# The first groups of a dense layer in wavefront order instead of three passes, with weight conversion paced to use (mLSTM cell and shrink layer, one core)

## The chip, the cores and the metric

The kernel runs on one core of a Trainium2 chip. A core has a matrix engine (TensorE, PE in the profile, with its weight loads as PEld), VectorE (DVE), ScalarE (ACT), GpSimd (POOL) and SyncE (SP), which here only issues transfers. Each engine works through its own list of instructions in order and waits on semaphores for the others. The metric is the device time of one execution in microseconds (us).

## The reference

An mLSTM cell runs over 4 batches, 8 heads, 768 steps and head size 40; its output, 3072 tokens of 320 features, goes through a dense layer with 2048 hidden features and the activation `h - tanh(h)`.

```python
for t in range(S):
    m_new = np.maximum(f_gate[:, :, t] + m, i_gate[:, :, t])
    f_stab = np.exp(f_gate[:, :, t] + m - m_new)
    i_stab = np.exp(i_gate[:, :, t] - m_new)
    C = f_stab * C + i_stab * einsum('bhd,bhe->bhde', v_t, k_t)
    n = f_stab * n + i_stab * k_t
    y[:, :, t] = sigmoid(o_gate_t) * (C @ q_t) / max(|n . q_t|, 1)
x = y.transpose(0, 2, 1, 3).reshape(B * S, H * D)   # 3072 x 320
h = x @ w_in                                        # 320 x 2048, float64 in memory
out = (h - tanh(h)) @ w_out                         # 2048 x 320, float64 in memory
```

All arithmetic on the chip is float32. The two weight matrices lie in memory as float64 bits and are turned into float32 on the chip.

## The kernel before

**Units.** The recurrence is done in chunks of 128 steps. A unit is one chunk of one batch, all heads: 24 units, numbered so that the four batches of a chunk follow each other. `cell_slot(s, o, x)` (line 435) makes a list of small steps for three units at once: unit `s` is fetched ahead, its decay matrix `E` is made by a scan on DVE (`decay`, line 341), and its scores are multiplied on PE into `ps` and from there by DVE into `E` (`score`, line 375); unit `o` gets its output `ph` from the state and from `E` (`inter`, `intra`), a state update `pc` (`update`, line 410) with DVE, and its output gate on DVE (`gate`, line 398); unit `x` is transposed on PE into `px` and copied by ACT into `xT` (`turn`, line 425). `prepare` (line 353) runs before an output: GpSimd scales `v` into `vs` and `q` into `qg`. `ph`, `pc` and `px` share one pool of two PSUM buffers (`ps_b`). The list `slots` (line 539) says which units a slot takes: normally `s`, `s-2` and `s-3`. There are 27 slots; a full one has all three units.

**Dense items.** Two units make a group of 256 tokens (12 groups); 256 hidden features make a weight pair (8 pairs). An item is one group with one pair: 96 items. `up(g, p)` (line 471) does six products into `ph_up` and the activation (two ACT and two DVE instructions into `gt`). `down(g, p, first, last)` (line 494) multiplies `gt` with `w_out` into the two accumulators `po`; it is issued `LAG` = 2 items after its `up`. `first` and `last` bound the run of pairs that one accumulation covers. At a run's end `evict` takes `po` out: ACT copies a group's first run into `part`, DVE adds later runs to `part`, and the last one goes to `ob` and to memory. Each of the two `po` has one buffer, so the next run's first product into it waits for that.

**Conversion.** `weights` (line 260) turns one float64 block into float32 in five pieces: a fetch by SP into the staging tile `w64` (six buffers); a mask and a shift on DVE (lines 282, 285); three ACT conversions (283, 286, 287); an add and a multiply on GpSimd (288, 289); and the sign on DVE (293). A pair has five blocks (three of `w_in`, two of `w_out`), 40 in all. `convert` (line 300) puts them into steps: step n fetches block n, does the middle of block n-2 and the sign of block n-4.

**Order.** PE's order is the order in which the program writes its products (`T.keep`). `merge` (line 523) interleaves two lists of steps in proportion to the costs that stand beside them. On the other engines the compiler orders the instructions by the program's order and its own estimate of when each is ready, so that a ready conversion can be put ahead of its place. The list before is in three passes over the first six groups: pairs 0 and 1 for groups 0 to 5, then pairs 2 to 4, then pairs 5 to 7; groups 6 to 11 then run all eight pairs each.

```python
PASSES = ((0, 1), (2, 4), (5, NP - 1))
```

Four slots and the conversion of pairs 0 and 1 (14 steps) come ahead of the first item. Slots 4 to 16 lie in items 0 to 11, together with the conversion of pairs 2 to 4; that of pairs 5 to 7 is laid over items 12 to 28; slots 17 to 26 lie in items 33 to 83.

Of the kernel before, what the change touches and what calls it, by code (L numbers as in the profile page):

```python
# [33 lines left out]
I64 = mybir.dt.int64  # L37
# [23 lines left out]
def kernel(  # L61
# [16 lines left out]
    class T:  # L78

        last = None  # L80
# [16 lines left out]
    B, NT, D, H, _ = qT.shape  # L97
# [4 lines left out]
    KC = [(c, min(128, DM - c)) for c in range(0, DM, 128)]  # L102
    NK = len(KC)
    NU = B * NT
    GT = 2
    TG = GT * L
    NG = NU // GT
    NP = NFF // 2
    HH = H // 2
    LAG = 2  # L110
    FIRST = 6
    NX = FIRST + 1
    PASSES = ((0, 1), (2, 4), (5, NP - 1))

    const = ctx.enter_context(tc.tile_pool(name="const", bufs=1))
    load = ctx.enter_context(tc.tile_pool(name="load", bufs=2))
# [2 lines left out]
    conv = ctx.enter_context(tc.tile_pool(name="conv", bufs=2))  # L119
# [85 lines left out]
    for w in (after, ones):  # L205
        p = ps_b.tile([w.shape[1], NT, BH], FP, name="psum_lf", tag="b")
# [12 lines left out]
    xr, n, f = (mlp.tile([L, 2, NR], FP, name=name, tag=tag) for name, tag in (("xr", "z"), ("n", "z"), ("f", "q")))  # L219
# [40 lines left out]
    def weights(dst, src):  # L260

        p, n = dst.shape
        w = {}

        def fetch():
            if src.dtype == FP:
                nc.sync.dma_start(out=dst, in_=src)
                return
            w["st"] = conv.tile([128, n], I64, name="w64", tag="w64", bufs=6)[0:p]
            nc.sync.dma_start(out=w["st"], in_=src)  # L270

        def magnitude():
            if src.dtype == FP:
                return
            hi = w["hi"] = w["st"].bitcast(I32).rearrange("p (n two) -> p n two", two=2)[:, :, 1]
            lo = w["st"].bitcast(U32).rearrange("p (n two) -> p n two", two=2)[:, :, 0]
            e = conv.tile([128, n], I32, name="w_e", tag="w_e")[0:p]
            m = conv.tile([128, n], I32, name="w_m", tag="w_m")[0:p]
            r = w["r"] = conv.tile([128, n], I32, name="w_r", tag="w_r", bufs=4)[0:p]
            mf, rf = m.bitcast(FP), r.bitcast(FP)  # L280

            V.tensor_single_scalar(e, hi, 0x7FF00000, op=OP.bitwise_and)  # L282
            A.activation(out=e, in_=e, func=AF.Relu, scale=8.0, bias=rebias[0:p])  # L283

            V.tensor_single_scalar(m, hi, 12, op=OP.logical_shift_left)  # L285
            A.activation(out=mf, in_=m.bitcast(U32), func=AF.Copy, scale=2.0 ** -32, bias=1.0)  # L286
            A.activation(out=rf, in_=lo, func=AF.Copy, scale=2.0 ** -52)
            G.tensor_tensor(out=rf, in0=rf, in1=mf, op=OP.add)  # L288
            G.tensor_tensor(out=rf, in0=rf, in1=e.bitcast(FP), op=OP.mult)  # L289

        def sign():
            if src.dtype != FP:
                V.scalar_tensor_tensor(out=dst.bitcast(I32), in0=w["hi"], scalar=-(1 << 31), in1=w["r"],  # L293
                                       op0=OP.bitwise_and, op1=OP.bitwise_or)

        return fetch, magnitude, sign

    WB = 2 * 128

    def convert(pairs):  # L300

        blocks = []
        for p in pairs:
            cols = slice(p * WB, (p + 1) * WB)
            for c, (r0, rows) in enumerate(KC):
                blocks.append(weights(w_in[0:rows, c, cols], moe_w_in[r0:r0 + rows, cols]))
            for f in (2 * p, 2 * p + 1):
                blocks.append(weights(w_out[:, f, :], moe_w_out[f * 128:(f + 1) * 128, :]))
        steps = []
        for x in range(len(blocks) + 4):  # L310
            def step(x=x):
                for late, part in enumerate((0, None, 1, None, 2)):
                    if part is not None and 0 <= x - late < len(blocks):
                        blocks[x - late][part]()
            steps.append((1.0, step))
        return steps


    xT = [const.tile([128, NK, TG], FP, name=f"xT{i}") for i in range(NX)]
    part = [const.tile([L, DM], FP, name=f"part{i}") for i in range(FIRST * GT)]  # L320

# [103 lines left out]
    def turn(n, j):  # L425
# [4 lines left out]
        if j == NK - 1:  # L430
            g, tt = divmod(n, GT)
            A.copy(out=xT[g % NX][:, :, tt * L:(tt + 1) * L], in_=t["px"])  # L432
            un.pop(n)

    def cell_slot(s, o, x):


        steps = []

        def begin():  # L440
            if o is not None:
                prepare(o)
            if s is not None and s - 1 in un:
                prepare(s - 1)
            if s is not None:
                if s + 1 < NU:
                    fetch(s + 1)
                decay(s)

        steps.append((0.0, begin))  # L450
        for d in range(HH):
            for i in range(2):
                if s is not None:
                    steps.append((0.22, lambda h=2 * d + i: score(s, h)))
                if o is not None and i == 0:
                    steps.append((0.22 if o >= B else 0.0, lambda d=d: inter(o, d)))
            if o is not None:
                steps += [(0.22, lambda h=h: intra(o, h)) for h in (2 * d, 2 * d + 1)]
                if d in (1, 2) and o + B < NU:
                    steps += [(0.18, lambda j=j: update(o, j)) for j in (2 * d - 2, 2 * d - 1)]  # L460
        if o is not None:
            steps.append((0.0, lambda: gate(o)))
        if x is not None:
            steps += [(0.11, lambda j=j: turn(x, j)) for j in range(NK)]
        return steps
# [57 lines left out]
    def merge(a, b):  # L523

        total = [sum(cost for cost, _ in x) or 1.0 for x in (a, b)]
        done, at = [0.0, 0.0], [0, 0]
        while at[0] < len(a) or at[1] < len(b):
            i = int(done[1] / total[1] < done[0] / total[0])
            if at[i] == len((a, b)[i]):
                i = 1 - i  # L530
            cost, step = (a, b)[i][at[i]]
            done[i] += cost
            at[i] += 1
            step()
# [1 line left out]

    slots = [(0, None, None), (1, 0, None), (2, 1, 0), (3, None, 1)]
    AHEAD = len(slots)  # L540
    slots += [tuple(n if lo <= n < NU else None for n, lo in ((s, 0), (s - 2, 2), (s - 3, 2)))
              for s in range(AHEAD, NU + 3)]
    NS = len(slots)

    def slots_for(g):

        return AHEAD if g == 0 else GT * g + 5

    items = []
    starts = {}  # L550
    for first, last in PASSES:
        for g in range(FIRST):
            starts[g, first] = len(items)
            items += [(g, p, first, last) for p in range(first, last + 1)]
    for g in range(FIRST, NG):
        starts[g, 0] = len(items)
        items += [(g, p, 0, NP - 1) for p in range(NP)]


    work = [[] for _ in range(len(items) + LAG)]  # L560

    def spread_over(steps, x0, x1):

        for i, step in enumerate(steps):
            work[int(x0 + i * (x1 - x0) / len(steps))].append(step)

    def pairs_of(i):
        return range(PASSES[i][0], PASSES[i][1] + 1)

    for g in range(FIRST):  # L570
        x0, now, then = starts[g, 0], slots_for(g), slots_for(g + 1)
        for i in range(now, then):
            n = len(pairs_of(0))
            spread_over(cell_slot(*slots[i]), x0 + (i - now) * n / (then - now), x0 + (i + 1 - now) * n / (then - now))
    for i in range(1, len(PASSES)):
        spread_over(convert(pairs_of(i)), starts[0, PASSES[i - 1][0]], starts[0, PASSES[i][0]] - 1)
    late = range(slots_for(FIRST), NS)
    x0, x1 = starts[1, PASSES[-1][0]], starts[NG - 1, 0] - HH
    for i, n in enumerate(late):
        spread_over(cell_slot(*slots[n]), x0 + (x1 - x0) * i / len(late), x0 + (x1 - x0) * (i + 1) / len(late))  # L580

    blocks = convert(pairs_of(0))
    spread(ld[0].setdefault("E", att.tile([L, H, L], FP, name="E", tag="E", bufs=4)), f_rows, 0, slice(0, H))
    for i in range(AHEAD):
        merge(cell_slot(*slots[i]), blocks[i * len(blocks) // AHEAD:(i + 1) * len(blocks) // AHEAD])
    for x in range(len(items) + LAG):
        dense = up(*items[x][:2]) if x < len(items) else []
        if x >= LAG:
            dense = dense + down(*items[x - LAG])
        merge(dense, work[x])  # L590


    most = att.tile([128, 1], FP, name="most", tag="most")
# [6 lines left out]
    lead, root, _, rest = POLY  # L600
# [17 lines left out]
    with tc.If(nc.values_load(again, min_val=0, max_val=128,  # L618
                              skip_runtime_bounds_check_because="it counts partitions") > 0):
        T.last = None  # L620
        for g in range(NG):
# [16 lines left out]
            x = xT[g % NX]  # L638
# [59 lines left out]
```

## Time and profile before

| what | us |
|---|---|
| median of 4 runs (lowest, highest) | 681.49 (679.31, 682.75) |
| the profiled execution, its time | 678.71 |
| the profiled execution, its span | 677.0 |
| PE busy, share of the span | 607.3, 90% |
| DVE busy, share | 365.4, 54% |
| ACT busy | 220.2 |
| POOL busy | 152.0 |
| first product of item 0, of item 12, of item 33, of item 84 | 59.93, 209.12, 323.35, 608.90 |

The profile is of one execution. Its span runs from the first to the last instruction; the execution's own time is 1.7 us longer. Matrix products are pipelined, so a busy PE is not one at its peak. The row of slices cuts the span in 40 parts of 16.9 us; a digit is the busy share in tenths, and PEclk is the clock that TensorE was granted, in tenths of full speed. In a line of a group of instructions, the numbers after the first bar are the busy time in us and the mean duration of one in ns, those after the second the time its engine stood idle right before these instructions and what ended most of it. In a line of the timeline, the first number is the start in us, the second how long the merged instructions last, and the bracket an idle time before them and its releaser.

### The profile page before, as it was taken

To read this page: it belongs to the slowest core of one execution; us is meant where nothing else is said; L and a number is where in the kernel's file an instruction comes from. 1 tells how busy PE (TensorE), PEld (TensorE's weight loads), DVE (VectorE), ACT (ScalarE), POOL (GpSimd) and SP (SyncE) were. 2 spreads that over 40 slices of the span, in tenths; PEclk is the share of its full clock that TensorE was granted. 3 is DMA by queue.
4 is the path that set the end of the run, shared out by engine and by line. 5 is a ranking of instruction groups with operands and counts; after the bars stand their busy time and mean duration, and the time that the engine had idled before them with its cause. 6 is when DMAs were issued, how large, how long until landed. Compare 5 with 4: busy or idle time off the path is not lost.

```text
span 677.0 us, 8514 instructions
## 1 busy us (share of the span) xinstructions
PE 607.3 (90%) x3100; PEld 504.3 (74%) x3100; DVE 365.4 (54%) x609; ACT 220.2 (33%) x511; POOL 152.0 (22%) x171
## 2 busy tenths in 40 slices
PE   1296889889899849999999999999999999999996
PEld 1295868778788637878888888888888888878784
DVE  8787888886887983333353635344333332332321
ACT  2333153243324743232232323222232322242331
POOL 7654355346354770000010101101010000000000
PEclk9757889899999979999999999999999999999999
DMA  5555765555344520000030402112000000000000
GB/s 156 174 159 178 214 187 148 160 153 157 119 134 140 167 86 1 0 1 0 20 99 29 133 13 93 56 36 79 1 11 19 1 1 19 1 21 0 20 0 25
DMA packets 46210, 50.97 MB, mean 75 GB/s; under 512 B 3984, under 2 KB 38416, under 8 KB 46160
## 3 DMA queue, kind: packets, MB, share of 16 engines
q1 hardware_dynamic: 42288, 46.22, 22.8%
q10 hardware_dynamic: 3872, 4.13, 1.8%
q8 instruction: 26, 0.43, 0.2%
q14 instruction: 24, 0.20, 0.1%
HBM read 46.20 MB, written 4.13 MB: 74 GB/s over the span
## 4 chain that ended last, share of the span: by engine, by line
PE 68%; DVE 15%; POOL 9%; issue 3%; ACT 3%; ACTq 0%; POOLq 0%; DVEq 0%
PE ph_up L91 32%; PE po L91 27%; DVE E L350 4%; PE ph L91 4%; PE ps L91 3%; POOL w_r L289 3%; POOL w_r L288 3%; DVE w_in L293 2%; DVE E L381 2%; DVE w_e L282 1%; ACT w_e L283 1%; DVE gt L489 1%; DVE w_out L293 1%; PE pc L91 1%; DVE w_m L285 1%
## 5 line engine op out<-in xcount | busy, mean ns | idle before, releaser
L91 PE MATMUL ph_up<-xT,w_in 128*128 128x256 f32 x1152 | 301.8, 388 | 5.5 <-ACT xT L432 3.7
L91 PE MATMUL po<-w_out,gt 128*128 128x320 f32 x768 | 246.8, 446 | 10.2 <-DVE part L508 8.5
L91 PEld LDWEIGHTS ph_up<-xT,w_in 128*128 128x128 f32 x1152 | 206.1, 192 | 38.9 <-ACT xT L432 5.4
L91 PEld LDWEIGHTS po<-w_out,gt 128*128 128x128 f32 x768 | 138.4, 194 | 48.1 <-DVE part L508 9.8
L489 DVE SCALAR_TENSOR_TENSOR gt<-ph_up,z 128x512 f32<-128x512 f32 x96 | 66.0, 688 | 198.2 <-ACT z L487 198.1
L487 ACT ACTIVATE z<-ph_up 128x512 f32<-128x512 f32 x96 | 57.2, 596 | 317.9 <-PE ph_up L91 316.1
L91 PE MATMUL ps<-q,kz 128*128 128x128 f32 x384 | 80.5, 309 | 11.1 <-DVE E L381 10.8
L91 PEld LDWEIGHTS ps<-q,kz 128*128 128x128 f32 x384 | 69.8, 215 | 18.9 <-DVE E L381 11.1
L490 DVE SCALAR_TENSOR_TENSOR gt<-q,gt 128x512 f32<-128x512 f32 x96 | 68.2, 710 | 9.0 <-ACT q L488 1.7
L91 PEld LDWEIGHTS ph<-vs,E 128*128 128x128 f32 x384 | 66.6, 205 | 7.5
L488 ACT ACTIVATE q<-z,tiny 128x512 f32<-128x512 f32 x96 | 69.2, 721 | 2.7
L350 DVE TENSOR_TENSOR_SCAN E<-E,diag 128x1024 f32<-128x1024 f32 x24 | 59.5, 2484 | 3.2 <-DMA E<-f_rows 3.2
L91 PE MATMUL ph<-vs,E 128*128 128x41 f32 x384 | 59.8, 261 | 0.0
L366 POOL TENSOR_TENSOR qg<-qg,q 80x512 f32<-80x512 f32 x20 | 26.2, 1311 | 138.3 <-DMA qg<-g_rows 138.3
L370 POOL TENSOR_TENSOR state<-state,eT 80x328 f32<-80x328 f32 x16 | 13.6, 849 | 158.1 <-PE ph L91 98.7
L381 DVE TENSOR_TENSOR E<-ps,E 128x512 f32<-128x512 f32 x48 | 32.8, 684 | 20.8 <-PE ps L91 19.3
L288 POOL TENSOR_TENSOR w_r<-w_r,w_m 128x256 f32<-128x256 f32 (+2 forms) x40 | 33.5, 837 | 41.3 <-ACT w_m L286 34.5
L289 POOL TENSOR_TENSOR w_r<-w_r,w_e 128x256 f32<-128x256 f32 (+2 forms) x40 | 36.3, 907 | 2.4
L91 PEld LDWEIGHTS ph<-state,qg 128*128 128x128 f32 x160 | 28.9, 194 | 5.8 <-POOL state L370 0.6
L293 DVE SCALAR_TENSOR_TENSOR w_in<-w,w_r 128x256 int32<-128x256 int32 (+1 forms) x24 | 25.8, 1074 | 13.5 <-POOL w_r L289 13.5
L95 PE MATMUL px<-ident,ys 128*128 128x128 f32 x72 | 16.1, 290 | 18.2 <-DVE state L421 14.2
L363 POOL TENSOR_TENSOR vs<-v,ei 128x640 f32<-128x640 f32 (+1 forms) x24 | 28.5, 1188 | 1.1 <-ACT z L487 0.5
(89 smaller groups left out, 356.4 us busy)
## 6 DMA issues: line engine op xcount, KB each, us to landing
E<-f_rows SPq DMA_DIRECT2D x24, 512.0 KB
w<-in_moe_w_out SPq DMA_DIRECT2D x16, 320.0 KB
w<-in_moe_w_in SPq DMA_DIRECT2D x16, 256.0 KB
kz<-in_kT SPq DMA_DIRECT2D x48, 80.0 KB
q<-in_qT SPq DMA_DIRECT2D x48, 80.0 KB
v<-in_v SPq DMA_DIRECT2D x24, 160.0 KB
k<-in_k SPq DMA_DIRECT2D x24, 160.0 KB
o<-in_o_gate SPq DMA_DIRECT2D x24, 160.0 KB
```

What stands on the lines that cost most here:

```text
L91: return cls.keep(nc.tensor.matmul(*args, **kwargs))
L288: G.tensor_tensor(out=rf, in0=rf, in1=mf, op=OP.add)
L289: G.tensor_tensor(out=rf, in0=rf, in1=e.bitcast(FP), op=OP.mult)
L293: V.scalar_tensor_tensor(out=dst.bitcast(I32), in0=w["hi"], scalar=-(1 << 31), in1=w["r"], op0=OP.bitwise_and, op1=OP.bitwise_or)
L350: V.tensor_tensor_scan(out=row, data0=row, data1=diag.rearrange("p h t -> p (h t)"), initial=0.0, op0=OP.mult, op1=OP.add)
L363: G.tensor_tensor(out=t["vs"][:, both, :, 0:D], in0=t["v"].unsqueeze(1).to_broadcast(shape), in1=scale.unsqueeze(3).to_broadcast(shape), o ...
L366: G.tensor_tensor(out=t["qg"][0:TOP], in0=t["qg"][0:TOP], in1=t["q2"][0:TOP], op=OP.mult)
L381: V.tensor_tensor(out=P, in0=t["ps"], in1=P, op=OP.mult)
L487: A.activation(out=z, in_=ph, func=AF.Square, accum_out=sums[:, g * NP + p:g * NP + p + 1])
L488: A.activation(out=q, in_=z, func=AF.Square, bias=tiny)
L489: V.scalar_tensor_tensor(out=gt, in0=ph, scalar=TINY_POLY[0], in1=z, op0=OP.mult, op1=OP.mult)
L490: V.scalar_tensor_tensor(out=gt, in0=q, scalar=TINY_POLY[2], in1=gt, op0=OP.add, op1=OP.mult)
```

## The change

The first four groups take the place of the first six. The list of items is written out as stages; each is a list of runs (group, first pair, last pair) and the number of cell slots laid over them. A new pair is used for all groups that are there, and a new group runs over all pairs that are there: item 0 is group 0 with pair 0, then group 0 with pair 1, group 1 with pairs 0 and 1, pair 2 for groups 0 and 1, and so on up to item 31. Groups 0 to 3 have 7, 6, 4 and 3 runs; before, six groups had three each. Groups 4 to 11 run all eight pairs each, as groups 6 to 11 did.

The slots are filled differently at the start: unit 2's output moves from slot 4 into slot 3, ahead of item 0, unit 3's into slot 4, and slot 5 has none. Slots 4 to 13 lie in the stages, 14 to 26 evenly over items 32 to 83, four items each. The conversion is one chain of 44 steps over all pairs. Nine steps, up to the end of pair 0, come ahead of item 0; five for each further pair are spread between the due times of the pair before and its own. Worked out, pair 1 is converted over item 0, pair 2 over items 1 and 2, pair 3 over 3 to 5.5, pair 4 over 5.5 to 11.5, pair 5 to 18, pair 6 to 20.5 and pair 7 to 27.5. Within an item, steps of cell and conversion are sorted by their place. The staging tile has eight buffers for six, there are six `xT` tiles for seven, and eight `part` tiles for twelve.

```diff
-    FIRST = 6
-    NX = FIRST + 1
-    PASSES = ((0, 1), (2, 4), (5, NP - 1))
+    STAGES = (
+        ([(0, 0, 0)], 2),
+        ([(0, 1, 1), (1, 0, 1)], 0),
+        ([(0, 2, 2), (1, 2, 2)], 1),
+        ([(0, 3, 3), (1, 3, 3)], 2),
+        ([(2, 0, 3)], 0),
+        ([(0, 4, 4), (1, 4, 4), (2, 4, 4)], 2),
+        ([(3, 0, 4)], 0),
+        ([(0, 5, 6), (1, 5, 6), (2, 5, 6), (3, 5, 6)], 2),
+        ([(0, 7, 7), (1, 7, 7), (2, 7, 7), (3, 7, 7)], 1),
+    )
+    FIRST = 4
+    NX = FIRST + 2
...
-            w["st"] = conv.tile([128, n], I64, name="w64", tag="w64", bufs=6)[0:p]
+            w["st"] = conv.tile([128, n], I64, name="w64", tag="w64", bufs=8)[0:p]
...
-    slots = [(0, None, None), (1, 0, None), (2, 1, 0), (3, None, 1)]
-    AHEAD = len(slots)
-    slots += [tuple(n if lo <= n < NU else None for n, lo in ((s, 0), (s - 2, 2), (s - 3, 2)))
-              for s in range(AHEAD, NU + 3)]
+    slots = [(0, None, None), (1, 0, None), (2, 1, 0), (3, 2, 1), (4, 3, 2), (5, None, 3), (6, 4, None)]
+    AHEAD = 4
+    slots += [tuple(n if n < NU else None for n in (s, s - 2, s - 3)) for s in range(len(slots), NU + 3)]
...
-    for first, last in PASSES:
-        for g in range(FIRST):
-            starts[g, first] = len(items)
+    for runs, _ in STAGES:
+        for g, first, last in runs:
             items += [(g, p, first, last) for p in range(first, last + 1)]
+    START = len(items)
...
+    x, done = 0, AHEAD
+    for runs, n in STAGES:
+        x1 = x + sum(last - first + 1 for _, first, last in runs)
+        for i in range(n):
+            spread_over(cell_slot(*slots[done]), x + i * (x1 - x) / n, x + (i + 1) * (x1 - x) / n)
+            done += 1
+        x = x1
+    x1 = (NG - 1 - FIRST) * NP - HH
+    for i in range(done, NS):
+        spread_over(cell_slot(*slots[i]), START + x1 * (i - done) / (NS - done), START + x1 * (i + 1 - done) / (NS - done))
...
+    steps = convert()
+    ready = [len(KC) * p + 2 * p + len(KC) + 2 + 4 for p in range(NP)]
+    due = [0.0, 1.0] + [min(i for i, item in enumerate(items) if item[1] == p) - 0.5 for p in range(2, NP)]
+    for p in range(NP - 2, 0, -1):
+        due[p] = max(min(due[p], due[p + 1] - 2.5), 1.0)
+    for p in range(1, NP):
+        spread_over(steps[ready[p - 1]:ready[p]], due[p - 1], due[p])
+
+    first = steps[:ready[0]]
...
-        merge(dense, work[x])
+        merge(dense, [(cost, step) for _, cost, step in sorted(work[x], key=lambda w: w[0])])
```

More of the change, by code (lines that the diff above doesn't have):

```diff
@@ L298, with convert @@
     WB = 2 * 128
-    def convert(pairs):
+    def convert():
         blocks = []
-        for p in pairs:
+        for p in range(NP):
             cols = slice(p * WB, (p + 1) * WB)
@@ L534, in merge @@
             step()
-    slots = [(0, None, None), (1, 0, None), (2, 1, 0), (3, None, 1)]
-    AHEAD = len(slots)
-    slots += [tuple(n if lo <= n < NU else None for n, lo in ((s, 0), (s - 2, 2), (s - 3, 2)))
-              for s in range(AHEAD, NU + 3)]
+    slots = [(0, None, None), (1, 0, None), (2, 1, 0), (3, 2, 1), (4, 3, 2), (5, None, 3), (6, 4, None)]
+    AHEAD = 4
+    slots += [tuple(n if n < NU else None for n in (s, s - 2, s - 3)) for s in range(len(slots), NU + 3)]
     NS = len(slots)
-    def slots_for(g):
-        return AHEAD if g == 0 else GT * g + 5
     items = []
-    starts = {}
-    for first, last in PASSES:
-        for g in range(FIRST):
-            starts[g, first] = len(items)
+    for runs, _ in STAGES:
+        for g, first, last in runs:
             items += [(g, p, first, last) for p in range(first, last + 1)]
+    START = len(items)
     for g in range(FIRST, NG):
-        starts[g, 0] = len(items)
         items += [(g, p, 0, NP - 1) for p in range(NP)]
@@ L562, in spread_over @@
     def spread_over(steps, x0, x1):
[L564 to L582, printed above, removed]
+        for i, (cost, step) in enumerate(steps):
+            at = x0 + i * (x1 - x0) / len(steps)
+            work[int(at)].append((at, cost, step))
+    x, done = 0, AHEAD
[16 more added lines that the diff above has]
+    first = steps[:ready[0]]
     spread(ld[0].setdefault("E", att.tile([L, H, L], FP, name="E", tag="E", bufs=4)), f_rows, 0, slice(0, H))
     for i in range(AHEAD):
-        merge(cell_slot(*slots[i]), blocks[i * len(blocks) // AHEAD:(i + 1) * len(blocks) // AHEAD])
+        merge(cell_slot(*slots[i]), first[i * len(first) // AHEAD:(i + 1) * len(first) // AHEAD])
     for x in range(len(items) + LAG):
```

## The prediction

> **What bounds the kernel now.** I read the page's shares and its row of 40 slices first, then the busy times by stretch, then the groups of instructions by shape, last the timeline of PE. The shares alone mislead: PE is busy 90% of the span, VectorE (DVE) 54%.
>
> ```profile
> PE 607.3 (90%) x3100; PEld 504.3 (74%) x3100; DVE 365.4 (54%) x609; ACT 220.2 (33%) x511; POOL 152.0 (22%) x171
> ...
> PE   1296889889899849999999999999999999999996
> ...
> DVE  8787888886887983333353635344333332332321
> ...
> PEclk9757889899999979999999999999999999999999
> ```
>
> The rows show two regimes: up to about slice 15 (250 us) DVE is at eight to nine tenths and PE has holes; from there PE is full and DVE has a third. So I cut the span where items of the dense list begin on PE: item 0 at 59.93 us, item 6 at 138.02, item 12 at 209.12, item 18 at 252.20, item 33 at 323.35, item 84 at 608.90 (starts of the first `ph_up` product of each, timeline of PE).
>
> ```profile
> core 0: us, PE busy (x) PEld busy (x) DVE busy (x) ACT busy (x) POOL busy (x), PEclk, DMA share, GB/s
> 20.00:60.00 40.00, 21.31 (x117) 20.50 (x116) 33.50 (x57) 14.78 (x38) 21.36 (x26) 0.66 0.59 184
> 60.00:138.00 78.00, 68.55 (x442) 60.46 (x443) 64.54 (x107) 24.26 (x65) 35.36 (x36) 0.91 0.61 172
> 138.00:209.00 71.00, 63.68 (x426) 55.24 (x425) 55.30 (x91) 25.10 (x64) 33.19 (x34) 0.98 0.51 155
> 209.00:253.00 44.00, 32.13 (x127) 24.20 (x126) 38.88 (x63) 27.90 (x70) 32.53 (x33) 0.92 0.37 114
> 253.00:323.00 70.00, 70.00 (x297) 56.16 (x296) 25.95 (x43) 21.14 (x45) 0.01 (x1) 1.00 0.00 1
> 323.00:609.00 286.00, 286.00 (x1421) 235.75 (x1421) 113.66 (x189) 82.26 (x182) 13.61 (x13) 1.00 0.12 37
> ```
>
> From 253 us on PE never stops. The prices on PE come from there. Items 18 to 32 start 4.743 us apart: that is a dense item. Items 33 to 63 take 174.55 us for 30 items, 32.3 us over 30 x 4.743, and hold 5.88 cell slots: **5.5 us of PE for a full slot**. With these prices items 0 to 11 and their 13 slots need 56.9 + 71.5 = 128.4 us and take 149.2; items 12 to 17 need 28.5 and take 43.1. These 35 us, and the 60 us before item 0, are all that can be had. The largest piece is one wait behind the conversion, which the pass before it had pulled ahead of its use:
>
> ```profile
> 236.63 2.86 PE L91 MATMUL ph_up<-xT,w_in 128*128 128x256 f32 x12 [1.69 <-DVE gt L489]
> 248.00 4.36 PE L91 MATMUL po<-w_out,gt 128*128 128x320 f32 x8 [8.51 <-DVE part L508]
> ```
>
> The prices on DVE, from the groups by shape (mean ns before the last bar):
>
> ```profile
> L490 DVE SCALAR_TENSOR_TENSOR gt<-q,gt 128x512 f32<-128x512 f32 x96 | 68.2, 710 | 9.0 <-ACT q L488 1.7
> L489 DVE SCALAR_TENSOR_TENSOR gt<-ph_up,z 128x512 f32<-128x512 f32 x96 | 66.0, 688 | 198.2 <-ACT z L487 198.1
> L350 DVE TENSOR_TENSOR_SCAN E<-E,diag 128x1024 f32<-128x1024 f32 x24 | 59.5, 2484 | 3.2 <-DMA E<-f_rows 3.2
> L381 DVE TENSOR_TENSOR E<-ps,E 128x512 f32<-128x512 f32 x48 | 32.8, 684 | 20.8 <-PE ps L91 19.3
> L421 DVE SCALAR_TENSOR_TENSOR state<-pc,own,state 80x164 f32<-80x164 f32 x32 | 11.7, 377 | 13.3 <-PE pc L91 13.2
> L293 DVE SCALAR_TENSOR_TENSOR w_in<-w,w_r 128x256 int32<-128x256 int32 x16 | 15.0, 938 | 9.6 <-POOL w_r L289 9.6
> ```
>
> A unit costs DVE 2.48 (scan), 1.37 (two score products), 1.67 (gate: 0.158, 0.156, 0.197, 0.670, 0.486) and 0.75 (two state updates): 6.3 us. A dense item costs 1.40. A weight block costs 1.96: lines 282, 285 and 293 are busy 17.7, 20.7 and 39.9 us for 40 blocks.
>
> **The change part by part.** *Shorter preamble.* Nine conversion steps in place of 14 take five blocks, 9.8 us of DVE, out of what lies before item 0. Moving unit 2's output there puts a gate and two state updates (2.4 us) and some 3 us of PE, about half a slot, in, and a wait: `px` of unit 1 now queues on PE behind `ph` and `pc` of unit 2, and all three share two buffers of `ps_b`, released by DVE's gate and state. One `xT` memset fewer takes 0.73 us off POOL's row of 5.1 us. Bounds for item 0: 9.8 us earlier to 5 us later; I take 60, no shift, since the next bound makes it immaterial.
>
> *The front, items 0 to 7.* What must be through DVE before item 8 can follow: nine scans 22.4, nine units' score products 12.3, seven gates 11.7, seven units' updates 5.3, eight items 11.2, six partial sums at 0.48 2.9, and 22 blocks (pairs 0 to 3, and two of pair 4) 43.1: 108.9 us. PE needs less there: 8 x 4.743 + about 4.5 full slots x 5.5 = 62.7 us. So DVE is the bound. How fast it goes through such a mixture, the trace shows: by 138 us it had done 11 scans, 22 score products, about 8.5 gates, 18 updates, 6 items and about 18 blocks, at these prices 107 us in the 118 us from 20 us on, 0.91 of the time. Item 8 then starts at 20 + 108.9 / 0.91 = 140 us. Ends: 0.85 gives 148, the 0.98 of the conversion stretch 209 to 253 (43.1 us of instructions in 44) gives 131.
>
> *Items 8 to 31* hold slots 9 to 13: PE 24 x 4.743 + 5 x 5.5 = 141.3 us. DVE has about 111 there: 24 items 33.6, five units 31.5, 18 blocks 35.3, some 22 partial sums 10.6. PE is the bound, and the conversion, paced over items 5.5 to 27.5, lies beside it; if that cover goes, it costs what the 43.1 us for items 12 to 17 show, 14.6. What PE loses: items 12 to 14 have two slots, PE 25 and DVE 24 us, the balance of 138 to 209, where need over time is 61.5 / 71.1 = 0.87: 3.7 us. Groups 2 and 3 start right behind the last transpose of their `xT`, so PE waits for ACT's copy (0.475): 1 us each. Run ends: 20 in these 32 items, 18 before over 48. All but four now end in DVE additions that stand in its order behind scans of 2.5 us; the next run may not write `po` before. The cover is the next item's `up`, 2.59 us; 13 of them lie in this part; I take 5 us, ends 0 and 23 (a scan, two score products and the addition, 4.3 us, less the 2.59, at each). Together 11: item 32 at 140 + 141.3 + 11 = 292.3.
>
> *From item 32 on* 52 items and 13 slots replace 51 items and 10 slots. Before: 285.55 us for items 33 to 83, of that 241.9 dense and 43.7 slots. After: 246.6 + 43.7 + 3 x 5.5 = 306.8. A slot per 4 items instead of 5.1 leaves DVE 12 of 24 us, so it is hidden. Then the same 12 items and end: 677.0 - 608.9 = 68.1.
>
> *Queues.* SP's fetches of weights spread out (24 of about 0.46, 16 of 0.36 us issue, the same number in all); in item 0 five of them stand between two units' loads of about 5 us of issue each, 12 us of SP in an item that holds 21 us of DVE's work. Eight staging buffers instead of six cost nothing in time. POOL and ACT keep their work, and no stretch shows them above three quarters.
>
> Sum: 292.3 + 306.8 + 68.1 = 667.2 span. The profiled execution took 678.71, 1.7 over its span, so 668.9; that is 9.8 less. The median of the four runs is 2.8 above the profiled one: **671.7**.
>
> **The rivals** (times on the median's scale).
>
> *Better coupling:* front at 0.98 of DVE, 5 us lost behind it: 131 + 141.3 + 5 + 374.9 + 4.5 = 657. For it: DVE has independent work at hand everywhere. Against: only a pure conversion stretch reached 0.98.
>
> *Nothing gained:* items 8 to 31 keep the 0.87 of 138 to 209: 141.3 / 0.87 = 162.4, item 32 at 302.4, end 681.8. For it: in-order DVE delayed `px` at nearly each slot there. Against: those stretches held six slots in six items; now it is five in 24.
>
> *Slower, the conversion as a wait:* in the front each pair is finished right before its use, so PE stands at items 1, 4 and 6 for DVE's last sign, and that stands for POOL's line 289. Before, DVE idled 9.6 + 11.6 + 3.9 = 25.1 us for it over 40 blocks, 0.63 each. A block alone runs through 0.45 + 0.5 (ACT) + 0.8 + 0.95 (POOL) + 0.94 us, of which DVE idles ACT's and POOL's 2.25 less its own 0.52 on line 285: 1.7. With nothing else in between, 22 blocks cost 22 x 1.07 = 23.7 more: 695. It decides once a block's idle time has about doubled: 13.2 us, the gain and half a per cent, over 22. For it: the chain that ended last goes through POOL's lines 363 and 288 into line 293 and the scan, slot after slot. Against: in 209 to 253 us 15 blocks came 2.9 us apart with DVE at 0.98, so the pieces of several blocks fill each other's gaps.
>
> *Slower, the clock:* PE's need in the front is 62.7 of 80 us, more holes than in 60 to 138 (67 of 78, clock 0.91). At the 0.66 of 20 to 60 it is 95 us, item 8 comes 15 us later: 687. After the 8.51 us hole above, the row of slices shows clock 7 in that slice. The Trainium skill (TensorE: Matmul & The Clock Gate, HAM oscillation) states that idle gaps over about 3.4 us put the clock to half; by that rule holes spread in pieces of 1 to 3 us, as here before, cost little, and only long waits for a pair make this case.
>
> **How the numbers follow.** Chances: forecast 0.43 (its own range 664 to 678, from 0.97 and 0.86 in the front), better coupling 0.15, nothing gained 0.15, conversion wait 0.20, clock 0.07. Half a per cent, 3.4 us, is about what a measurement of this kernel can tell from no change: faster 0.58, same 0.15, slower 0.27. Below 655 lies half of better coupling; above 690 over half of the conversion wait: the range is 655 to 690.
>
> **What would show it.** Right: DVE near nine tenths and PE with holes only up to about 140 us; item 8 at 131 to 148, item 32 at 285 to 300; POOL busy past 200 us; no single 8 us wait for `part`. Wrong: PE waits that end with DVE `w_in` (conversion), `part` waits over 1.5 us at most run ends, clock rows of 6 or less past 60 us, or item 32 after 302.

## The result and the profile after

The changed kernel takes 681.36 us (median of 41 runs, 679.13 to 683.47), the kernel before, in its 67 runs, 680.38. The ratio is 1.0012 with a 95% interval of 1.0006 to 1.0019: no change that matters, where 671.7 and a range of 655 to 690 were forecast, with 0.15 on "same". The profiled execution has a span of 678.0 us against 677.0.

From the page of the changed kernel, the shares and some rows of its 40 slices:

```profile
PE 610.7 (90%) x3100; PEld 508.5 (75%) x3100; DVE 363.3 (54%) x617; ACT 223.1 (33%) x511; POOL 157.8 (23%) x170
...
PE   1388678797689999999999999999999999999996
...
DVE  8688878967876235665553553454353333332321
...
POOL 7535657754732010220220120111011000000000
PEclk9998979789979999999999999999999999999999
```

PE has no hole from slice 12 on (about 205 us); before, from slice 15 on. It is full from item 15 at 206 us on, where item 18 at 252 us began that before and holes only up to about 140 us were forecast. The end does not move, since 15 items and 7 of the slots from 4 on lie behind PE by then, not 18 and 13. The row of POOL points to what happened: GpSimd's part of the conversion was to be spread to item 27, which is 273 us here, and it is over after slice 11. The busy times by stretch, cut where items begin (item 0 at 59.13, item 8 at 145.09, item 15 at 205.69, item 32 at 303.19, item 84 at 610.09):

```profile
core 0: us, PE busy (x) PEld busy (x) DVE busy (x) ACT busy (x) POOL busy (x), PEclk, DMA share, GB/s
20.00:59.00 39.00, 26.18 (x139) 25.25 (x138) 30.26 (x51) 9.83 (x27) 17.41 (x20) 0.96 0.55 165
59.00:145.00 86.00, 66.47 (x356) 56.64 (x356) 71.61 (x126) 41.21 (x103) 51.55 (x53) 0.88 0.53 156
145.00:206.00 61.00, 48.08 (x243) 39.36 (x244) 46.63 (x85) 28.52 (x72) 34.42 (x36) 0.92 0.35 105
206.00:303.00 97.00, 97.00 (x492) 80.13 (x491) 47.63 (x79) 27.53 (x61) 12.69 (x10) 1.00 0.18 58
303.00:610.00 307.00, 307.00 (x1593) 254.85 (x1592) 133.33 (x217) 91.09 (x200) 25.78 (x23) 1.00 0.16 50
```

With the forecast's prices (4.743 us a dense item, 5.5 a full slot), what PE needs and what it took:

| stretch | need | before | after | forecast for after |
|---|---|---|---|---|
| to item 0 | | 59.9 | 59.1 | 60 |
| items 0 to 11 / 0 to 7 | 128.4 / 62.7 | 149.2 | 86.0 | 80 |
| items 12 to 17 / 8 to 14 | 28.5 / 44.2 | 43.1 | 60.6 | about 50 |
| items 18 to 32 / 15 to 31 | 71.1 / 97.1 | 71.1 | 97.5 | about 102 |
| from there to item 84 | | 285.6 | 306.9 | 306.8 |
| to the end of the span | | 68.1 | 67.9 | 68.1 |

Before, PE lost 35 us behind item 0; after, 40: 23 in items 0 to 7 and 16 in items 8 to 14, against some half a slot that was moved into the preamble. About half of the 16 us is one wait at item 13. On the timeline of PE:

```profile
188.72 0.66 PE L96 MATMUL px<-ident,ys 128*128 128x128 f32 x2 [8.35 <-DVE state L434]
```

The transpose waits for two state updates on DVE. The products that these take in, `pc`, were done on PE at 177.5 us. What DVE did ahead of the updates, on its timeline:

```profile
179.27 0.80 DVE L295 TENSOR_SCALAR w_e<-w 128x256 int32<-128x256 int32 x1 [0.76 <-POOL w_r L302]
179.99 0.48 DVE L306 SCALAR_TENSOR_TENSOR w_out<-w,w_r 128x320 int32<-128x320 int32 x1
180.39 0.68 DVE L394 TENSOR_TENSOR E<-ps,E 128x512 f32<-128x512 f32 x1
181.09 0.80 DVE L295 TENSOR_SCALAR w_e<-w 64x256 int32<-64x256 int32 x1
...
182.02 0.94 DVE L306 SCALAR_TENSOR_TENSOR w_in<-w,w_r 128x256 int32<-128x256 int32 x1
...
184.47 2.05 DVE L503 SCALAR_TENSOR_TENSOR gt<-q,gt 128x512 f32<-128x512 f32 x1
186.44 0.98 DVE L298 TENSOR_SCALAR w_m<-w 128x320 int32<-128x320 int32 x1
187.34 0.31 DVE L295 TENSOR_SCALAR w_e<-w 128x320 int32<-128x320 int32 x1
187.57 0.41 DVE L306 SCALAR_TENSOR_TENSOR w_in<-w,w_r 64x256 int32<-64x256 int32 x1
187.91 0.67 DVE L434 SCALAR_TENSOR_TENSOR state<-pc,own,state 80x164 f32<-80x164 f32 x2
```

These are blocks of the last pairs, 6 and 7, whose places are items 18 to 27, standing ahead of what item 13 needs. The last sign starts at 191 us. The compiler had put the conversion ahead of its place, as it had done before the change (last sign at 253 us, its place being item 28, which begins at 300 us there).

### The profile page after: what moved, and what is told of

Same layout as the page of the kernel before. It is cut to its first block, busy times and chain, and to the rows that moved or that the text cites. A ratio compares the mean times of both kernels' runs of the same rounds, so it can differ in the third digit from the quotient of the medians.

```text
span 678.0 us, 8577 instructions
## 1 busy us (share of the span) xinstructions
PE 610.7 (90%) x3100; PEld 508.5 (75%) x3100; DVE 363.3 (54%) x617; ACT 223.1 (33%) x511; POOL 157.8 (23%) x170
## 4 chain that ended last, share of the span: by engine, by line
PE 77%; DVE 9%; POOL 4%; DMA 3%; issue 3%; ACT 2%; SPq 1%; ACTq 0%; POOLq 0%; DVEq 0%
PE ph_up L92 34%; PE po L92 28%; PE ph L92 6%; PE ps L92 6%; POOL w_r L301 2%; POOL w_r L302 2%; DMA w<-in_moe_w_in 2%; DMA E<-f_rows 2%; PE pc L92 2%; DVE E L363 1%; PE px L96 1%; DVE gt L503 1%; DVE w_e L295 1%; DVE w_out L306 1%; DVE w_m L298 1%
## 5 line engine op out<-in xcount | busy, mean ns | idle before, releaser
L92 PE MATMUL ph_up<-xT,w_in 128*128 128x256 f32 x1152 | 317.8, 395 | 9.7 <-DVE gt L502 4.7
L92 PE MATMUL po<-w_out,gt 128*128 128x320 f32 x768 | 252.4, 442 | 3.9 <-DVE part L521 3.9
L92 PEld LDWEIGHTS ph_up<-xT,w_in 128*128 128x128 f32 x1152 | 202.4, 194 | 37.3 <-DVE gt L502 5.3
L92 PEld LDWEIGHTS po<-w_out,gt 128*128 128x128 f32 x768 | 132.8, 192 | 33.2 <-DVE part L521 4.7
L500 ACT ACTIVATE z<-ph_up 128x512 f32<-128x512 f32 x96 | 57.2, 596 | 255.1 <-PE ph_up L92 255.0
L92 PEld LDWEIGHTS ps<-q,kz 128*128 128x128 f32 x384 | 74.5, 218 | 21.1 <-DVE E L394 8.9
L92 PEld LDWEIGHTS ph<-vs,E 128*128 128x128 f32 x384 | 71.7, 208 | 10.4 <-issue 0.5
L363 DVE TENSOR_TENSOR_SCAN E<-E,diag 128x1024 f32<-128x1024 f32 x24 | 55.9, 2331 | 8.5 <-DMA E<-f_rows 8.5
L376 POOL TENSOR_TENSOR vs<-v,ei 128x640 f32<-128x640 f32 (+1 forms) x24 | 28.5, 1190 | 127.3 <-PE ph L92 122.9
L379 POOL TENSOR_TENSOR qg<-qg,q 80x512 f32<-80x512 f32 x20 | 35.5, 1777 | 10.1 <-DMA qg<-g_rows 6.2
L92 PEld LDWEIGHTS pc<-vs,k 128*80 128x80 f32 x160 | 22.9, 168 | 20.0 <-issue 8.2
L92 PE MATMUL pc<-vs,k 128*80 128x82 f32 x160 | 25.2, 259 | 11.6 <-DVE ys L421 8.9
```

The lines of the kernel that those rows point to most:

```text
L92: return cls.keep(nc.tensor.matmul(*args, **kwargs))
L363: V.tensor_tensor_scan(out=row, data0=row, data1=diag.rearrange("p h t -> p (h t)"), initial=0.0, op0=OP.mult, op1=OP.add)
L376: G.tensor_tensor(out=t["vs"][:, both, :, 0:D], in0=t["v"].unsqueeze(1).to_broadcast(shape), in1=scale.unsqueeze(3).to_broadcast(shape), o ...
L379: G.tensor_tensor(out=t["qg"][0:TOP], in0=t["qg"][0:TOP], in1=t["q2"][0:TOP], op=OP.mult)
L500: A.activation(out=z, in_=ph, func=AF.Square, accum_out=sums[:, g * NP + p:g * NP + p + 1])
```

## The experiments

**Keeping the conversion at its place.** PE's order is fixed by hand; DVE's is not. The edit fixes a part of it: a conversion's instruction on DVE may not be put ahead of the last DVE instruction of another kind (of the cell or of a dense item) that is written ahead of it. Nothing else changes, and no wait is taken away. In both kernels:

```diff
+    class Mark:
+        last = None
+        def __getattr__(self, name):
+            def call(*args, **kwargs):
+                i = getattr(nc.vector, name)(*args, **kwargs)
+                Mark.last = i
+                return i
+            return call
+    V = Mark()
+    def behind(i):
+        if Mark.last is not None:
+            tc.add_manual_dep(i.ins, Mark.last.ins.name, NO_SYNC, reason="conversion keeps its place")
...
-            V.tensor_single_scalar(e, hi, 0x7FF00000, op=OP.bitwise_and)
+            behind(nc.vector.tensor_single_scalar(e, hi, 0x7FF00000, op=OP.bitwise_and))
... (the same for the shift and the sign)
```

> The changed kernel with one edit: each conversion instruction on VectorE is kept behind the VectorE instruction that is written ahead of it, so that the conversion lies where the list of items puts it (the last sign at item 27 instead of item 13). Theory A (the compiler pulls the conversion ahead of its paced place, and items 8 to 15 pay for it): the 16 us that items 8 to 15 lose on PE fall to under 6, the last sign comes past 260 us, and the whole takes 665 to 672 us. Theory B (the loss comes from the cell slots themselves, whose score products, gates and state updates stand in VectorE's order in front of what PE waits for): items 8 to 15 keep over 10 us of loss and the time stays within 3 us of the changed kernel, 678 to 684.

Measured 668.26 us, ratio 0.9825 (0.9801 to 0.9848) to the kernel before on the same chip. The last sign comes at 256 us, short of the 260 expected; items 8 to 14 take 49.7 us where they took 60.6, a loss of 5.5 instead of 16.4; items 0 to 7 stay at 85.7. Theory A holds, B falls. This is the kernel the forecast had described: item 32 comes at 292.2 us, where 292.3 was forecast, and the median stands 3.4 us from the forecast of 671.7. Part of that is luck, since two errors cancel: items 0 to 7 take 85.7 us instead of 80, and items 15 to 31 take 97.7 instead of about 102.

> The kernel before with the same edit (conversion kept behind what is written ahead of it on VectorE). Theory A: the 14.6 us that items 12 to 17 lose disappear, items 0 to 11 stay as they are: 666 to 671 us. Theory B: nothing moves by more than 3 us.

Measured **647.74 us**, ratio 0.9529 (0.9513 to 0.9545): far more than either theory gave. The loss of items 12 to 17 is gone (28.5 us for 28.5 needed), but so is that of items 0 to 11: 129.9 us for 128.4 needed, where 149.2 were taken. The stretches of this kernel:

```profile
62.00:192.00 130.00, 127.88 (x867) 114.64 (x868) 117.48 (x198) 50.66 (x128) 91.71 (x70) 0.96 0.68 189
192.00:292.00 100.00, 100.00 (x425) 80.19 (x424) 54.68 (x106) 49.30 (x115) 29.60 (x33) 1.00 0.18 52
```

PE and DVE are now both above nine tenths in the first of them, side by side. Items 6 to 11, from which the forecast had read its ratio of 0.87 between need and time, take 61.5 us here for 61.5 needed. So that ratio, called the balance of a stretch there, was not one of the mixture but of the order.

**Without the arithmetic of the conversion.** Each block is written by one ScalarE copy; magnitudes, signs and GpSimd's part are left out, so the weights are not those of the reference.

> The changed kernel with the arithmetic of the conversion left out: each weight block is fetched as before and written by one ScalarE copy of its low halves, so VectorE and GpSimd do nothing for it and the weights are wrong. Theory A (the conversion's share of VectorE is what holds items 0 to 15): VectorE's work for items 0 to 7 falls from 109 to 66 us, about PE's 63, item 8 comes at 125 to 132 us and no loss stays behind it: 645 to 656 us. Theory B (cell slots): item 8 moves by less than 8 us, the time stays over 668 us.

> The kernel before with the arithmetic of the conversion left out in the same way. Theory A: items 12 to 17 lose nothing and items 0 to 11 go from 149 to 130 to 140 us: 644 to 656 us, about as much as the changed kernel gains. Theory B: only the 14.6 us of items 12 to 17 go, items 0 to 11 stay at 145 to 150: 662 to 668 us, and the changed kernel without conversion is faster than this by over 8 us.

Measured 642.37 us (0.9457, 0.9438 to 0.9476) and 638.29 us (0.9389, 0.9351 to 0.9427). In the changed kernel item 0 comes at 57.3 and item 8 at 118.1 us, 60.8 us for a need of 62.7: no loss at all, earlier than theory A had it. In the kernel before item 0 comes at 53.2, items 0 to 11 take 128.2. Both times lie below what theory A gave. The conversion is what holds both, and with it out of the way the wavefront is 4 us slower: its item 0 comes 4.1 us later. Behind item 0 both orders have about the same work for PE (580.5 and 582.0 us to the end of the span), so a change of order can gain there only time that is lost.

**Which piece of the conversion.** The edit above, for the sign alone and for mask and shift alone, in the kernel before.

> The kernel before; only the sign, the last of the three VectorE pieces of a block, is kept behind what is written ahead of it; mask and shift are free. In the held kernel the 16 signs between items 0 and 12 take 8.6 us of VectorE (0.54 us each), in the kernel before 25 us (1.6 us each), while mask and shift cost about the same. Theory C (the sign is what hurts: pulled ahead, it runs beside GpSimd's add and multiply of the next block and is drawn out, and VectorE's list stands behind it): as fast as the fully held kernel, 646 to 652 us. Theory D (mask and shift hurt, by taking VectorE at the wrong time): 665 to 680 us.

> The kernel before; mask and shift are kept behind what is written ahead of them, the sign is free to come as early as the compiler finds it ready. Theory C: the signs between items 0 and 12 stay at 1.2 us or more each and items 0 to 11 take 142 us or more: 658 to 672 us. Theory D: 646 to 652 us.

Measured 655.08 us (0.9636, 0.9610 to 0.9661) with the sign held and 690.17 us (1.0142, 1.0117 to 1.0167) with mask and shift held. Holding the sign brings 25 us of the 32.4, 3 us short of theory C's range; 4.9 us are still lost in items 0 to 11 and 5.9 in items 12 to 17, of which 1.5 remain with mask and shift held as well. Holding those two without the sign makes the kernel slower than it was, where both theories had it faster. The waits of DVE for GpSimd, from the list of who waited for whom (us in total, times, longest), first of the kernel before, then with mask and shift held, then with the sign held:

```profile
DVE w_in L293 <- POOL w_r L289: 13.5, 10, 2.2
DVE w_out L293 <- POOL w_r L289: 11.6, 7, 2.6
```

```profile
DVE w_in L310 <- POOL w_r L306: 31.5, 17, 2.3
DVE w_out L310 <- POOL w_r L306: 24.5, 13, 2.7
```

```profile
DVE w_out L310 <- POOL w_r L306: 1.1, 1, 1.1
```

25.1, 56.0 and 1.1 us: the sign that comes too early stops DVE, in order, until GpSimd has multiplied, and everything behind it stands. How that looks, from the timeline of the kernel before (DVE and POOL at item 7):

```profile
153.65 0.99 DVE L293 SCALAR_TENSOR_TENSOR w_out<-w,w_r 128x320 int32<-128x320 int32 x1 [1.36 <-POOL w_r L289]
...
155.73 0.72 POOL L289 TENSOR_TENSOR w_r<-w_r,w_e 128x256 f32<-128x256 f32 x1
156.41 1.26 POOL L366 TENSOR_TENSOR qg<-qg,q 80x512 f32<-80x512 f32 x1
156.48 1.48 DVE L293 SCALAR_TENSOR_TENSOR w_in<-w,w_r 128x256 int32<-128x256 int32 x1 [1.83 <-POOL w_r L289]
157.88 2.28 DVE L350 TENSOR_TENSOR_SCAN E<-E,diag 128x1024 f32<-128x1024 f32 x1
```

DVE waits 1.83 us for `w_r`; then the sign takes 1.48 us, because GpSimd has gone on to `qg` 0.07 us before and the sign ends only behind it. Held back, most signs take 0.41 to 0.48 us. Both costs come together: the end of GpSimd's multiply releases the sign and lets GpSimd begin its next instruction, here 0.07 us apart. Of the 16 signs of items 0 to 11, the 14 for which DVE had waited over 0.7 us took 0.99 to 4.32 us, and each of them ends 0.28 or 0.35 us behind a GpSimd instruction; the other two took 0.43 and 0.47. So the early sign costs twice, by its wait and by its length; the runs do not part the two. The sign's own busy time from 60 to 209 us, in the kernel before and in the held one:

```profile
60.00:209.00 149.00, 24.95 (x16) 0.94 0.57 164
```

```profile
60.00:209.00 149.00, 9.87 (x19) 0.95 0.66 184
```

24.95 us for 16 signs, 9.87 for 19: 1.56 and 0.52 us each. That is 17 us of length, next to the 25 us of waits over the whole kernel; together more than the 35 us that PE lost, so not all of it reached PE. The Trainium skill (SBUF — State Buffer, Who interferes with whom) states that a VectorE instruction with two SBUF inputs contends with a GpSimd instruction that reads SBUF, and that the port pair they share is an exclusive lock. The trace agrees: the sign reads two such tiles and ends 0.3 us behind `qg`, which started first, and in the held kernel before it is GpSimd's add that is drawn out to 3.21 us beside a scan of 2.27.

**Where item 0 begins.** The edit, switched on only from the first dense item.

> The kernel before, held, but only from the first dense item on; the preamble is ordered as in the kernel before. Item 0 of the held kernel comes at 62.3 us, that of the kernel before at 59.9. If nothing else depends on it: item 0 at 59.5 to 60.5, items 0 to 11 in 130 us, 644.5 to 647 us. If the preamble's order has put conversions ahead that items 0 to 11 then miss, the gain is given back: 647 to 649.

Measured **644.47 us**, ratio 0.9471 (0.9448 to 0.9495), at the lower end of what was expected: item 0 at 59.8, items 0 to 11 in 129.9. Of the kernels that leave nothing out this is the fastest, 5.3% below the kernel before.

**Why the wavefront stays 20 us behind when both are held.** First its due places, moved ahead:

```diff
+    due[2:] = [2.5, 4.0, 8.0, 12.0, 17.0, 23.0]
```

> The changed kernel, held, with the due places of pairs 2 to 7 moved ahead by 0.5 to 4 items (2.5, 4, 8, 12, 17, 23). In the held kernel item 4 stands 8.27 us for the last sign of pair 2, items 6 and 7 lose 12 us. Theory E (the wait is one of latency: the pair is finished right before its use): items 1 to 7 lose 8 us less and the time is 656 to 663 us. Theory F (VectorE is full from item 0 on, so what is converted earlier delays something else by as much): 665 to 671 us.

Measured 664.70 us (0.9768, 0.9722 to 0.9813). Items 0 to 7 take 85.4 us after 85.7, so in the front nothing is gained, as Theory F had it, and a wait for the last sign of pair 2's `w_in` is still there, 6.5 us after 8.27; items 8 to 14 take 46.6 after 49.7. The time lies between the ranges of both theories, and its interval overlaps that of the held wavefront, so a gain of the whole is not shown. F's reason is not shown either: in the held wavefront DVE is busy for 66.9 of the 86 us of the front. Then the arithmetic of pairs 1 to 3 left out, and the slots laid apart (two short edits, in `weights` and in `STAGES`, where the counts of the first four stages become 2, 1, 1, 1):

> The changed kernel, held, with the arithmetic of the conversion left out for pairs 1 to 3 alone (one ScalarE copy in its place, so those weights are wrong); pairs 0 and 4 to 7 are converted as ever. It asks what the wavefront's front pays for. Theory G (items 0 to 7 lose 23 us because three pairs must be converted inside them): they fall from 85.7 to 62 to 68 us, the rest stays, and the time is 644 to 651 us. Theory H (they lose it to five cell slots bunched on few items): they stay over 78 us and the time over 660.

> The changed kernel, held, with slot 6 laid over items 1 to 3, which hold none, slot 7 over items 4 and 5 and slot 8 over items 6 and 7, so that no item of these holds more than half a slot. Theory H (bunched slots): items 0 to 7 lose 6 us less or better, 655 to 662 us. Theory G (the conversion in the front): the loss moves to other items, 665 to 671 us.

Measured 640.38 us (0.9394, 0.9358 to 0.9431) and 661.42 us (0.9703, 0.9675 to 0.9731). The stretch of items 0 to 7, first of the held wavefront, then of the one with pairs 1 to 3 cheap:

```profile
59.00:145.00 86.00, 69.00 (x357) 59.43 (x358) 66.89 (x119) 39.27 (x98) 50.24 (x51) 0.83 0.55 155
```

```profile
59.00:122.00 63.00, 60.73 (x358) 53.02 (x359) 45.61 (x76) 27.35 (x70) 24.91 (x21) 0.94 0.72 210
```

The same products on PE in 62.5 us instead of 85.7, with 21 us less of DVE; of the 23 us, some 15 are PE's idle time and 8 its longer busy time at the lower clock (0.83 for 0.94). Theory G holds, with 4 us more gained than it said: three pairs converted inside eight items are what the front pays for. Since the cheap blocks skip GpSimd and two of three ScalarE steps too (GpSimd 24.9 us for 50.2), the runs do not tell DVE's time from the chain through the three engines. The slots have a smaller part: laid apart, items 0 to 7 take 82.0 and items 8 to 14 take 47.2 us, so Theory H's time came, with 3.7 us of the 6 in the front where it had put all.

**The shorter preamble alone**, in the kernel before, held from item 0 on: the chain of conversion of the change, nine steps ahead of item 0, pair 1 over item 0, the passes as they were; then the same with passes of pairs 0-1, 2-3 and 4-7.

> The kernel before, held from the first item on, with the change's shorter preamble alone: one chain of conversion, nine steps ahead of item 0 and pair 1 over item 0, everything else as it was. It measures what five blocks fewer in the preamble are worth without unit 2's output moved into it (the prediction took 9.8 us of VectorE for them). If the preamble is VectorE's: item 0 at 52 to 56 us; items 0 to 11, where VectorE is at 0.98, then take 4 to 8 us longer, and the time is 642 to 646 us. If item 0 waits for the cell's chain: item 0 at 58 to 60 us, 645 to 650 us.

> As the run before, with pair 4's conversion and use moved from the second pass to the third (passes 0-1, 2-3, 4-7), so that items 0 to 11 carry 15 blocks again. If VectorE is the bound there: items 0 to 11 in 128 to 132 us with item 0 at 52 to 56, 636 to 641 us. If item 0 does not move: 644 to 648 us; more if the third pass's 20 blocks over 12 items leave PE waiting.

Measured 659.45 us (0.9682, 0.9661 to 0.9704) and 661.74 us (0.9724, 0.9702 to 0.9746), the first outside what was expected, the second only within its open end ("more if"), and both slower than the 644.47 they start from. Five blocks fewer bring item 0 from 59.8 to 57.2 us, 2.6 us for 9.8 us of DVE work. Items 0 to 3 then take 61.1 us where they took 48.0. In the second run items 0 to 3 are long as well (56.3), items 4 to 11 stand at their need, and item 16 takes 8.6 us more than a dense item in the denser third pass. In both, conversion beside the first items is worse placed than ahead of them.

## Why the prediction was wrong

*The step that failed* is in the part on items 8 to 31: "the conversion, paced over items 5.5 to 27.5, lies beside it". The list paces it; the compiler did not keep the pace. The conversion was done in item 13, and items 8 to 14 lost 16.4 us. Held to its place, they lose 5.5, about what the forecast had for them, so the early conversion cost 10.9 us there. Item 32 came late by as much, at 303.2 for 292.3 and past the sign of being wrong at 302, since 6 us too many in the front and 4.8 too few in items 15 to 31 nearly cancel. The prediction's own price for that case, "if that cover goes, it costs what the 43.1 us for items 12 to 17 show, 14.6", was near, but it stood there as a price without a chance. The row to see it in was at hand: before the change the last sign stood at 253 us, though the written place of its step was item 28, at 300 us, and the prediction named this very pulling ahead without asking what would stop it in the new kernel. Its sign "POOL busy past 200 us" did not come from the conversion: GpSimd's last multiply of a block starts at 190 us. Held to the written order, the changed kernel takes 668.3.

*The front* was forecast by DVE's work over 0.91: 80 us for items 0 to 7, measured 86.0, item 8 at 145.1 within the ends of 131 and 148. That the conversion makes the front long was right (62.5 us without pairs 1 to 3, held). That DVE's throughput is its bound did not come out: by item 8, 26 blocks had their sign instead of 22; held, it is 22, and the front is as long. DVE and PE are then each busy for about 0.8 of it, and PE's two longest holes (8.27 and 4.98 us) end with DVE. The price of a block, 1.96 us, also had the long signs in it; in the held kernel before the three pieces take 1.37. And 0.91 and 0.87 were taken as what such mixtures allow; held, items 0 to 11 of the kernel before give 0.99 on PE.

*The preamble:* item 0 at 59.1 for 60; the bound "9.8 us earlier" was far off, as the 2.6 us of the shorter preamble alone show. That item 0's shift was immaterial was wrong too: without the conversion it is about the whole difference of the two orders.

*Run ends:* 5 us were taken for 13 of them. Items 15 to 31 take 97.5 us for 97.1 needed, so they cost nothing there. In items 8 to 14 two waits of 1.62 and 2.29 us show on PE's timeline.

*The rest* held: 306.9 for 306.8 from item 32 to 84, 67.9 for 68.1 to the end, and the 5.5 us for a slot.

*The rivals.* "Nothing gained" gave 681.8 for 681.4, but that is luck: it had the loss spread over items 8 to 31, and it lay in 8 to 14 and in a front 6 us longer than forecast; from 15 on there was none. "The conversion as a wait" put PE behind a sign that comes late. In the changed kernel the signs come early, and it is DVE that stands for GpSimd (14.5 us in all) with PE behind it; PE itself waits for a sign of `w_in` once, for 3.2 us, and once for 8.27 us in the held wavefront. Its number of 25.1 us of DVE idle before signs was the right place to look: holding the sign brought 25 us in the kernel before, and it had been counted as part of a ratio. "The clock" asked for slices of 6 or less past 60 us, and none shows; with 0.88 in items 0 to 7, PE was busy for 66.5 us there for a need of 62.7, and for 47.8 for 44.2 in items 8 to 14, so a lower clock took at most some 4 us in each. Whether these reached the end was not tried. Its condition, gaps over 3.4 us, is not this trace's: in the kernel before the granted clock was 0.50 for 3.41 us each from 77.5, 98.0, 125.3 and 149.2 us on, beside single gaps of PE of 1.3, 2.9, 2.9 and 2.4 us.

## What to carry to other kernels

Where a compiler may reorder an engine's list, compare the time at which each piece ran with the place at which it was written before pricing a change of the written place; a pace that nothing enforces is a wish. An engine that works in order pays for a piece that comes too early as for one that comes too late: count what it idles before such pieces and how much longer they take than at their best, and hold them back before rearranging the work around them. And a ratio of need to time read off a stretch is a measurement of that order; it need not be a limit of the mixture.

## What the runs showed of the hardware

The same VectorE instruction (the sign of a block, 128x256) takes 0.41 us when no GpSimd instruction runs ahead of it, as in the held kernel before, and 1.48 us when GpSimd's `qg` starts 0.07 us ahead of it; it ends 0.3 us behind that instruction. Over 149 us of the kernel before, this and its like made 16 signs cost 24.95 us in place of 8.3 at the held rate of 0.52. We had not expected that holding back 40 instructions, each of under half a microsecond at its best, would be worth 25 us.
